# Stored sums for q and k, paired score adds and a replanned order in a Strassen-style attention and gated-MLP kernel

## The chip, the cores and the metric

The kernel runs on one core of one Trainium2 chip. The metric is device microseconds of one execution, lower is better; a version's time is the median of its runs. The core's engines are TensorE (PE, matmuls; PEld is its weight load), VectorE (DVE), ScalarE (ACT), GpSimd (POOL) and SyncE (SP). SP, POOL and ACT also issue DMAs, each in the order of its own queue; 16 DMA engines carry them.

## The reference

All inputs are bfloat16. `S` is 2048, `D` 1024, `F` 3584, 32 heads of 32, 8 offsets of step 2.

```python
xn = _layernorm(x)
qkv = (xn @ wqkv)                       # q, k, v by heads
idx = pos[:, None] - off[None, :]       # off = 0, 2, ... 14
kg, vg = k[:, :, idx_c], v[:, :, idx_c] # dilated window of 8 keys
logits = einsum("bhsd,bhswd->bhsw", q, kg) * scale   # masked where idx < 0
o = einsum("bhsw,bhswd->bhsd", softmax(logits), vg)
s = o @ wo
h = silu(xn @ w1) * (xn @ w3)
g = silu(h @ w2)
out = x + s * g
```

## The kernel before, in words

**Work and tiles.** The sequence is cut into four chunks of 512 rows (`CH`), two to a block (`BL` = 1024 rows, `NB` = 2 blocks; the code counts them as `b` = 0 and 1, the change's title calls the second "block 2"). Each large product is done on 2x2 blocks with seven products instead of eight, Strassen's way, so that some products take sums and differences of weights (`qkv_sums` L779, `w_sums` L1123, `w2_sums` L1212, `wo_sums`) and of activations (`xn_sums`, L461's helper `tt` issues them all on DVE). Within each block the order is: layer norm and the transposes of its output into `xT`; the q, k and v products (`qkv_pairs`); 14 steps of the gated up-projection (`up_step`, 256 columns of `w1` and `w3` each); the down-projection (`mlp_down`); and the output projection (`wo`). The attention itself has no matmul: scores, softmax and the weighted sum of values are elementwise DVE work that is placed beside PE's products, chunk by chunk (`scores` L866, `softmax`, `values`).

**Sums of weights.** In block 0 the sums are made on DVE; those that block 1 needs again are stored in DRAM from POOL's queue (`s_dram`, `s2_dram`, `t_dram`, `lt_dram`, and `sq_dram` for the q, k, v weights) and fetched by SP in block 1. For q, k and v the set `RL` (L354) says which of the three are stored: before, `RL = (2,)`, so v alone; the four sums of 128x2048 each of q and of k are made anew in block 1 from the weights, which are loaded in both cases.

**Scores.** `scores(c)` multiplies q with k shifted by each of the 8 offsets: two products of 128x2048 (`qk`), one add of 2048 (`qa`), one of 1024 (`qb`), one of 512 into `E` (`qc`). After four offsets `gather` brings the four partial sums of each head together by DMAs from `E` (two on POOL's queue, two on SP's), and `softmax` goes on with them. The `att` pool holds three buffers of 128x2048 for these and for the values.

**Buffers.** Weights and their sums share six buffers of 1 MB, the pool `r8` (the trace calls them `r`); `att` is `a`, `k2` (in the trace `k`) holds what ACT copies out of PSUM, `mm` is the eight PSUM banks. `h_sb` holds the up-projection's result, and before that, piece by piece, the `w2` weights whose sums go to `t_dram`, and parked q, k and v. A buffer is filled again when all users of what it held have ended, DMAs included.

**The order of the work.** Nothing is issued as the code runs. Each operation is recorded in `plan` with what it reads and writes, an assumed duration, and for DMAs their bytes. `limits` (L132) gives each a due time from the fixed order of PE's work. `simulate` (L158) then lets each engine take, of what is ready, the operation due first; DMAs share one pipe, each taking its bytes at one rate (`RATE` 3.3e5 bytes per us), the DMA's issue and 0.9 us. `replay` (L247) repeats this for each row of `ORDER`, which shifts due times of operations by number and moves PE's work, and the order that comes out last is what is issued; on the chip every engine keeps to it and waits by semaphores. All elementwise DVE work thus stands under one line, L461, all plain DMAs under L489, the matmuls of most products under L452, those of half width under L1099 and L1370, copies under L466, silu under L483 and the transposing DMAs under L654.

**The transposes.** `ln_turn` (L650) turns the next block's normalized rows into `xT` by transposing DMAs: four for chunk 2 on ACT's queue, four for chunk 3 on SP's. Each waits for a mark of the down-projection, after which its piece of `xT` is free.

Of the kernel before, what the change touches and what calls it, by code (L numbers as in the profile page):

```python
# [8 lines left out]
FP32 = mybir.dt.float32  # L9
# [25 lines left out]
class Op:  # L35
    __slots__ = ("eng", "emit", "rd", "wr", "occ", "lat", "table", "nbytes", "pred", "succ", "n",
                 "start", "done", "ready", "limit", "name", "late", "idx", "rate", "then", "need", "eta")


class Plan:  # L40
# [117 lines left out]
    def simulate(self):  # L158
# [24 lines left out]
        while left:  # L183
# [13 lines left out]
            if e == PE:  # L197
                o = ops[pes[pe_at]]
                pe_at += 1
                lag = T - o.need  # L200
            else:
                wait = None
                for i in sorted((i for i in ready[e] if ops[i].ready <= T), key=lambda i: (ops[i].limit, i)):
                    o = ops[i]
                    end = T + o.occ + (1.29 if o.table and o.table != table else 0.0)
                    hit = None
                    if e in self.look:
                        k = bisect.bisect_right(due[e], (T + 0.01, -1))
                        while k < len(due[e]) and due[e][k][0] < end - 0.05:
                            q = ops[due[e][k][1]]  # L210
                            k += 1
                            if q.start is None and q is not o and q.need < o.need:
                                hurt = end - max(q.need + lag, q.eta)
                                if hurt > 0.05 + self.look[e] * (q.eta - T):
                                    hit = q
                                    break
                    if hit is None:
                        break
                    wait = hit.eta if wait is None else min(wait, hit.eta)
                else:  # L220
                    free[e] = wait
                    continue
                ready[e].remove(i)
# [44 lines left out]
            o.emit()  # L268


ORDER = ((((403, 0.7), (402, -0.4), (438, 0.4), (402, -0.2), (409, -0.4), ), ()),
(((686, -1.1), (1076, 2.2), ), ((243, 242), )),
(((679, 2.4), (686, -1.6), (1076, 1.1), (680, 1.4), (680, 2.1), ), ((244, 242), )),
(((686, -0.4), (680, 1.1), (686, -0.6), ), ((245, 243), )),
(((998, -1.2), ), ()),
(((1077, 0.5), (1183, 1.2), ), ()),
(((1177, 0.7), (1178, 0.3), ), ()),
(((1183, 1.6), ), ()),
(((1181, 1.5), ), ((377, 376), )),
(((1077, 0.3), ), ((248, 247), )),  # L280
(((1284, -0.9), (1224, -0.8), (1128, 0.5), (1303, 1.2), ), ()),
(((1077, 0.2), (1200, 0.4), (714, 0.8), ), ((404, 403), )),
(((691, -0.3), ), ()),
(((1526, -1.5), (1529, 2), (1183, 0.8), (1183, 2), ), ()),
(((1548, 1.4), (1229, 0.2), ), ()),
(((694, 0.7), (993, 0.6), ), ((477, 471), )),
(((993, 0.9), (693, 0.6), (1545, 1.7), ), ((468, 472), )),
(((716, 0.2), (1199, 0.6), (715, -0.4), ), ()),
(((995, 0.6), ), ((251, 250), )),
(((1548, -0.6), (693, 0.2), (1231, 0.5), ), ((377, 371), )),  # L290
(((1181, 0.4), (691, -0.1), ), ((472, 471), )),
(((1554, 0.6), ), ()),
(((714, -0.4), (714, -0.1), (1463, 0.6), (1557, -1.2), ), ()),
(((702, 0.3), ), ()),
(((1545, -0.3), (693, 0.6), (686, 0.3), (1463, 0.6), (694, 0.7), ), ((478, 472), )),
(((1014, -1.3), (1222, 3.2), ), ()),
(((1526, 0.6), ), ()),
(((1520, 0.5), ), ()),
((), ((371, 370), (371, 370), )),
((), ((371, 370), (371, 370), )),  # L300
((), ((368, 371), (371, 370), )),
(((1446, 0.7), (1526, 0.6), (1470, 0.7), ), ()),
(((1245, -0.4), (1247, 0.9), (1247, 0.3), ), ((367, 371), )),
(((1212, 1.8), (1221, 1.7), ), ((371, 370), (364, 370), )),
(((1559, -0.3), ), ((369, 366), )),
(((1437, 0.8), (1575, -0.7), (1438, 1), (1528, 1), (1014, -1), ), ((485, 483), (366, 371), )),
(((2328, 2.3), ), ()),
(((1575, 2.8), (2022, 0.6), ), ((484, 483), )),
(((2085, 1), (1226, 0.7), (2087, -0.3), (1578, 1.8), ), ()),
(((1226, 0.8), ), ()),  # L310
(((1461, 2.7), ), ()),
(((1225, -0.3), (2093, -0.8), (2093, -0.6), ), ()),
(((1181, 0.6), (2090, 0.6), (1225, -0.4), ), ()),
(((2471, 0.3), ), ((475, 483), (483, 481), )),
(((1737, 0.7), (1519, -0.6), ), ((476, 475), )),
(((1737, 0.5), ), ((476, 483), (483, 481), )),
)
LAST = []

# [2 lines left out]
def kernel(  # L322
# [78 lines left out]
    LAST[:] = [plan]  # L401
    plan.pools = {
        "r8": [const.tile([P, 4 * D], BF16, name=f"r8_{i}") for i in range(6)],
        "att": [const.tile([P, 4 * CH], BF16, name=f"a4_{i}") for i in range(3)],
    }
    plan.wide = {"k2": const.tile([P, 8, CH], FP32, name="k2"), "mm": psum.tile([P, 8, CH], FP32, name="mm")}
    for n, t in plan.wide.items():
        plan.pools[n] = [t[:, i] for i in range(8)]

    ctx.enter_context(tc.manual_schedule())  # L410

# [74 lines left out]
    def dma(eng, name, o, a, rd, wr, kb, late=0.0):  # L486
        e = {SP: nc.sync, POOL: nc.gpsimd, ACT: nc.scalar}[eng]
        occ = {SP: 0.45, POOL: 0.58, ACT: 0.42}[eng]
        plan.op(eng, name, lambda: e.dma_start(out=o(), in_=a()), rd, wr, occ, 0.0, nbytes=kb * 1024, late=late)  # L489

    def sub_of(s, *idx):
        return (s,) + idx
# [157 lines left out]
    def ln_turn(c, st, xt, cell):  # L650

        half = c % 2
        eng, q, occ = (ACT, nc.scalar, 0.1) if c == 2 else (SP, nc.sync, 1.4)
        plan.op(eng, f"turn{c}_{st}", lambda: q.dma_start(  # L654
            out=xT[:, half, :, st * P:(st + 1) * P], in_=xrow(xt, st), transpose=True),
            [(xt, st), cell], xt_cells(half, 0, st) + xt_cells(half, 1, st), occ, 0.0, nbytes=256 * 1024)


    def qkv_load(t, split=False):
# [206 lines left out]
    def scores(c):  # L866
# [1045 lines left out]
```

## Time and profile before

| | |
|---|---|
| median of 3 runs | 713.04 us (712.6 to 715.51) |
| the profiled execution | 712.91 us, of which the span of its instructions is 711.1 |
| DMA | 165.68 MB, mean 233 GB/s |
| granted TensorE clock | 1.0 |
| matmul, 128x512 | drawn 379 ns long |
| DVE add, 128x2048 / 128x1024 / 128x512, all bf16 | 1213 / 680 / 413 ns |

The page's matmul ends are modelled: successive matmuls overlap as drawn, so a busy share near 100% says only that they follow one another closely. A DVE instruction is likewise drawn a little into the next one; start to start is what the engine needs. Times in the views are microseconds from the span's start.

### The profile page before, as it was taken

Reading aid. Unit: us, or ns where it says so; the run is one execution under the profiler, and the core shown is the slowest. Engines: PE = TensorE matmul, PEld = TensorE weight load, DVE = VectorE, ACT = ScalarE, POOL = GpSimd, SP = SyncE. Lnnn points to the kernel's source line nnn. Section 1 sums busy time; section 2 is a strip of 40 time slices with the busy share of each in tenths; the row PEclk is TensorE's granted clock in tenths of the full one; section 3 lists DMA queues with packets and bytes.
Section 4 is the critical chain, followed back from the end, with each engine's and each line's share of the span. In section 5 each row is a group of like instructions: output and inputs, shape, how many; then the busy total and the mean of one; then the engine's idle time right before and its main releaser. Section 6 shows DMA issues by size and latency. Waiting matters only on the chain.

```text
span 711.1 us, 9896 instructions
## 1 busy us (share of the span) xinstructions
PE 697.9 (98%) x3612; PEld 374.2 (53%) x3666; DVE 684.7 (96%) x859; ACT 397.6 (56%) x752; POOL 46.1 (6%) x89
## 2 busy tenths in 40 slices
PE   8999999999999999999999999999999999999997
PEld 5555545455555474644455554555555455656443
DVE  7999899999999999989999999999999999999965
ACT  7644565658565799512445455666866855322233
POOL 1011010112010010100010000000010010000000
PEclk9999999999999999999999999999999999999999
DMA  9999987666964779994466549973586575957502
GB/s 335 288 338 374 377 314 223 215 214 219 299 211 165 260 251 226 301 281 138 164 230 243 177 159 325 327 253 113 181 262 201 181 226 171 339 193 244 177 30 89
DMA packets 137087, 165.68 MB, mean 233 GB/s; under 512 B 16784, under 2 KB 112672, under 8 KB 131408
## 3 DMA queue, kind: packets, MB, share of 16 engines
q1 hardware_dynamic: 125552, 128.14, 56.5%
q0 software_dynamic: 6832, 35.41, 13.4%
q10 hardware_dynamic: 4656, 1.51, 1.3%
q8 instruction: 28, 0.46, 0.3%
q14 instruction: 19, 0.16, 0.1%
HBM read 113.12 MB, written 39.58 MB: 215 GB/s over the span
## 4 chain that ended last, share of the span: by engine, by line
PE 77%; DVE 14%; DMA 4%; issue 2%; ACT 2%; SPq 0%; DVEq 0%; ACTq 0%
PE mm L452 67%; PE mm L1099 5%; PE mm L1370 5%; DVE a L461 4%; DVE h_sb L461 3%; DVE r L461 3%; DMA h_sb<-in_B_w_dram 2%; DMA r<-in_B_w_dram 1%; DVE small L549 1%; DVE xs L461 1%; DMA r<-in_A_x_dram 1%; DVE r L565 0%; ACT k L466 0%; DVE k L461 0%; DMA xT<-r 0%
## 5 line engine op out<-in xcount | busy, mean ns | idle before, releaser
L452 PEld LDWEIGHTS <-r 128*128 128x128 f16 (+1 forms) x2068 | 219.4, 108 | 202.4 <-issue 4.9
L452 PE MATMUL mm<-xs,r 128*128 128x512 f16 x1280 | 300.3, 379 | 3.1 <-DVE h_sb L461 1.6
L452 PE MATMUL mm<-xT,r 128*128 128x512 bf16 (+2 forms) x747 | 173.2, 369 | 2.4 <-ACT small L554 0.2
L466 ACT COPY k<-mm 128x512 f32<-128x512 f32 (+1 forms) x226 | 124.3, 559 | 79.8 <-PE mm L452 72.8
L466 ACT COPY mm<-mm 128x512 f32<-128x512 f32 (+1 forms) x157 | 76.5, 491 | 108.3 <-PE mm L1099 34.0
L452 PE MATMUL mm<-r,h_sb 128*128 128x512 f16 (+1 forms) x583 | 129.2, 379 | 1.0 <-DMA r<-in_B_w_dram 0.5
L452 PEld LDWEIGHTS <-h_sb 128*128 128x128 f16 (+1 forms) x680 | 66.5, 98 | 80.5 <-issue 1.7
L461 DVE TENSOR_TENSOR a<-a,a 128x2048 bf16<-128x2048 bf16 (+3 forms) x70 | 78.4, 1122 | 0.2
L461 DVE TENSOR_TENSOR h_sb<-mm,k 128x1024 bf16<-128x1024 f32 x48 | 58.0, 1215 | 1.8 <-ACT k L466 1.1
L461 DVE TENSOR_TENSOR a<-qo,kT 128x2048 bf16<-128x2048 bf16 x48 | 57.7, 1215 | 0.1
L1099 PE MATMUL mm<-xT,r 128*128 128x256 f16 (+1 forms) x364 | 56.7, 273 | 0.0
L461 DVE TENSOR_TENSOR h_sb<-h_sb 128x1024 f16<-128x1024 bf16 (+7 forms) x74 | 53.4, 742 | 1.8 <-DMA h_sb<-in_B_w_dram 1.8
L461 DVE TENSOR_TENSOR r<-r,r 128x1024 f16<-128x1024 f16 (+7 forms) x62 | 50.0, 812 | 0.7 <-DMA xT<-r 0.5
L461 DVE TENSOR_TENSOR a<-E,vT 128x2048 bf16<-128x2048 bf16 x42 | 49.7, 1214 | 0.0
L1099 PEld LDWEIGHTS <-r 128*128 128x128 f16 (+1 forms) x364 | 35.6, 98 | 26.3
L461 DVE TENSOR_TENSOR k<-mm,k 128x1024 f32<-128x1024 f32 (+1 forms) x44 | 44.8, 1019 | 1.1 <-PE mm L452 0.8
L483 ACT ACTIVATE k<-k 128x512 bf16<-128x512 f32 x56 | 32.5, 626 | 20.1 <-DVE k L461 20.0
L483 ACT ACTIVATE h_sb<-mm 128x512 bf16<-128x512 f32 x60 | 36.4, 611 | 10.7 <-PE mm L452 9.3
L461 DVE TENSOR_TENSOR qo<-qo,a 128x2048 bf16<-128x2048 bf16 x32 | 38.8, 1213 | 0.0
L461 DVE TENSOR_TENSOR r<-r 128x1024 f16<-128x1024 bf16 (+4 forms) x73 | 38.1, 535 | 0.1
L461 DVE TENSOR_TENSOR h_sb<-h_sb,k 128x2048 bf16<-128x2048 bf16 x28 | 33.9, 1210 | 0.3 <-ACT k L483 0.3
L466 ACT CAST k<-mm 128x512 bf16<-128x512 f32 x56 | 31.5, 602 | 0.2 <-PE mm L452 0.2
(132 smaller groups left out, 563.9 us busy)
## 6 DMA issues: line engine op xcount, KB each, us to landing
r<-in_B_w_dram SPq DMA_DIRECT2D x42, 512.0 KB, 6.0
s_dram<-r POOLq DMA_DIRECT2D x14, 1024.0 KB, 5.1
r<-s_dram SPq DMA_DIRECT2D x14, 1024.0 KB, 5.0
r<-t_dram SPq DMA_DIRECT2D x15, 896.0 KB, 8.0
r<-in_A_wqkv_dram SPq DMA_DIRECT2D x10, 1024.0 KB, 7.1
r<-in_B_w_dram SPq DMA_DIRECT2D x11, 896.0 KB, 6.1
h_sb<-in_B_w_dram SPq DMA_DIRECT2D x14, 512.0 KB, 8.3
t_dram<-h_sb POOLq DMA_DIRECT2D x7, 1024.0 KB, 9.1
```

Source lines behind the costliest of these rows:

```text
L452: nc.tensor.matmul(cut(ps.ap()), lhsT=lhs[k](), rhs=cut(rhs[k]()), start=(first and k == 0), stop=(last and k == n - 1), skip_group_check= ...
L461: plan.op(DVE, name, lambda: fn(out=o(), in0=a(), in1=b()), rd, wr, occ, 0.08, late=late)
L466: plan.op(ACT, name, lambda: nc.scalar.copy(out=o(), in_=a()), rd, wr, occ, 0.11)
L483: plan.op(ACT, name, lambda: nc.scalar.activation(out=o(), in_=a(), func=ACTF.Silu), rd, wr, occ, 0.11, table="silu")
L549: plan.op(DVE, f"bn{c}_{st}_{h}", lambda h=h: nc.vector.bn_stats(out=stats[:, h, :], in_=xrow(xt, st)[:, h * 512:(h + 1) * 512]), ([("x ha ...
L1099: nc.tensor.matmul(half(pa[i].ap, n)(), lhsT=A[0][k](), rhs=B[0][k](), start=first and k == 0, stop=k == 1, skip_group_check=True)
L1370: nc.tensor.matmul(half(bank.ap, n)(), lhsT=a[k](), rhs=c[k](), start=first and k == 0, stop=k == NQ - 1, skip_group_check=True)
```

## The change

- `RL` becomes `(0,1,2)`: the sums for q and k are stored in DRAM in block 0, two stores of 1 MB each on POOL's queue, and fetched in block 1 by two DMAs of 1 MB each on SP's queue. The four sums each of q and k in block 1 are no longer made. The loads of the weights themselves stay.
- The three `att` buffers become one tile, so that two neighbours can be addressed together. In `scores`, for all offsets of chunks 2 and 3 and the first four of chunks 0 and 1, two offsets are taken together: products and `qa` as before, then one `qb` over both (128x2x1024) and one `qc` over both (128x2x4x128).
- The planner: each kind of DMA gets a factor on its bytes (`COST`), the fixed part of a DMA changes, `RATE` is 3.25e5, and a DMA is held back while the assumed pipe is over 4 us behind and the DMA is due in over 25 us.
- `ln_turn`: the transposes of chunk 3 also wait until all four of chunk 2 have landed; the assumed issue time and bytes are larger.
- `ORDER` is another list: 67 rows of shifts and moves instead of 46.

The two programs hold the same matmuls. In the new order of PE some groups of matmuls trade places in the first down-projection, the first output projection, the q and k products of block 1, one up step and the last output projection's neighbours; up to the first down-projection PE's order is the old one, and up to about 45 us that of DVE. On SP's queue seven instead of ten fetches of `w2` pieces stand ahead of the v weights; five of the 14 stand behind fetches for later up steps. On POOL's queue three instead of seven stores of `w2` sums stand ahead of the second store of up-projection sums; the four new stores stand first, third and so on among them.

```diff
+BACKLOG, SPARE = 4.0, 25.0
...
                     o = ops[i]
+                    if o.nbytes and pipe - T > BACKLOG and o.need + lag - T > SPARE:
+                        wait = T + 0.5 if wait is None else min(wait, T + 0.5)
+                        continue
...
-                pipe = max(pipe, T + occ + 0.9) + o.nbytes / o.rate
+                pipe = max(pipe, T + min(occ, 0.45) + 0.66) + o.nbytes / o.rate
...
-    RL = (2,)
+    RL = (0,1,2)
...
-        "att": [const.tile([P, 4 * CH], BF16, name=f"a4_{i}") for i in range(3)],
     }
-    plan.wide = {"k2": const.tile([P, 8, CH], FP32, name="k2"), "mm": psum.tile([P, 8, CH], FP32, name="mm")}
+    plan.wide = {"att": const.tile([P, 3, 4 * CH], BF16, name="a4"), "k2": const.tile([P, 8, CH], FP32, name="k2"), "mm": psum.tile([P, 8, CH], FP32, name="mm")}
...
+        for part, cost in COST:
+            if name.startswith(part):
+                kb = kb * cost
+                break
...
+    COST = (("turn", 1.7), ("w1.", 1.17), ("w3.", 1.17), ("putk", 1.14), ("putq", 1.35), ("put_s", 0.87), ("put_l", 1.43),
+            ("s_dram", 0.8), ("s2", 1.7), ("L", 0.58), ("E", 0.69), ("out", 0.65), ("t2_", 1.15), ("wo", 1.2),
+            ("getv", 1.21), ("get_l", 1.15), ("movev", 1.48))
...
-        eng, q, occ = (ACT, nc.scalar, 0.1) if c == 2 else (SP, nc.sync, 1.4)
+        eng, q, occ = (ACT, nc.scalar, 0.1) if c == 2 else (SP, nc.sync, 2.3)
...
-            [(xt, st), cell], xt_cells(half, 0, st) + xt_cells(half, 1, st), occ, 0.0, nbytes=256 * 1024)
+            [(xt, st), cell] + [("turned", k) for k in range(NST) if c == 3],
+            xt_cells(half, 0, st) + xt_cells(half, 1, st) + [("turned", st)] * (c == 2), occ, 0.0, nbytes=int(1.7 * 256 * 1024))
...
+        two = None
         for w in range(W):
...
+            if c >= 2 or w < 4:
+                if w % 2 == 0:
+                    two = plan.pair("att", f"p{c}_{w}", f"p{c}_{w}")
+            else:
+                two = None
             for jh in range(2):
-                p_t = plan.slot("att", f"p{c}_{w}_{jh}")
+                p_t = two[w % 2] if two and not jh else plan.slot("att", f"p{c}_{w}_{jh}")
...
+            if two and w % 2 == 0:
+                continue
+            if two:
+                v = lambda two=two: two[0].both().rearrange("p w (j n) -> p w j n", j=4)
+                tt(f"qb{c}", add, lambda v=v: v()[:, :, 0:2], lambda v=v: v()[:, :, 0:2], lambda v=v: v()[:, :, 2:4], two, two, 2048, True)
+                tt(f"qc{c}", add, lambda w=w: E[:, :, w - 1:w + 1, :].rearrange("p q w n -> p w q n"),
+                   lambda v=v: v()[:, :, 0].rearrange("p w (q n) -> p w q n", n=P),
+                   lambda v=v: v()[:, :, 1].rearrange("p w (q n) -> p w q n", n=P),
+                   two, [("E", x, sq, r) for x in (w - 1, w) for sq in range(4) for r in range(NR)], 1024, True)
+                if w % 4 == 3:
+                    gather(c, w // 4)
+                continue
...
-    RATE = 3.3e5
+    RATE = 3.25e5
```

More of the change, by code (lines that the diff above doesn't have):

```diff
@@ L268, in run @@
             o.emit()
[L271 to L292, printed above, removed]
@@ L316 @@
-(((1737, 0.5), ), ((476, 483), (483, 481), )),
+ORDER = (((), ((29, 26), (29, 26), (29, 26), (29, 26), )),
+((), ((27, 26), (27, 26), )),
+((), ((27, 26), (27, 26), )),
+(((647, -0.7), ), ()),
+(((684, 1.9), ), ()),
+(((684, 1.8), ), ()),
+((), ((243, 242), )),
+(((1076, 0.5), (684, 1.1), ), ((244, 242), )),
+(((684, 3.3), (684, 7.4), ), ((245, 243), )),
+(((1004, 1.1), (1175, 3.5), (1077, 0.7), ), ()),
+(((695, -0.4), ), ()),
+(((1074, 3.8), (1074, 5.3), (1077, 1.4), ), ((248, 247), )),
+(((1077, 0.3), ), ((251, 250), )),
@@ new lines @@
+(((1193, 10.9), (1193, 10.3), ), ()),
+((), ((375, 377), )),
+(((1012, 0.6), ), ((370, 369), )),
+(((1220, -0.3), ), ()),
+(((1175, 10.8), (1006, 0.2), (1175, 3.6), ), ((368, 371), )),
+(((1276, 0.4), ), ()),
+(((1126, 7.6), ), ((405, 403), )),
+(((1305, 4.1), (1350, -4.2), (1311, 3.1), (1277, 4.6), (1174, 0.3), ), ((423, 417), )),
+(((1347, 1.8), ), ((422, 417), )),
+(((1174, 0.4), (997, 8.3), (1344, 1), (1304, 0.4), ), ()),
+((), ((427, 426), )),
+(((1347, 1.4), ), ()),
+((), ((419, 417), )),
@@ new lines @@
+(((1174, 0.8), ), ()),
+(((1176, 0.6), (1012, -0.6), ), ()),
+(((1173, 0.3), (1004, 2), (1173, 0.4), (1174, 0.5), ), ()),
+(((1012, -0.4), (1012, -0.2), (1012, -0.5), (1173, 0.8), ), ()),
+(((1175, 0.5), ), ((377, 376), )),
+(((1012, -0.4), (1012, -0.2), ), ((369, 368), )),
+(((1472, 6.6), (1345, 0.5), (1343, 0.3), ), ()),
+(((1387, -0.6), (1343, 0.3), ), ((435, 434), )),
+((), ((27, 26), (27, 26), )),
+((), ((25, 26), (25, 26), )),
+((), ((458, 455), )),
+((), ((456, 455), (456, 455), )),
+((), ((458, 456), )),
@@ L317 @@
+((), ((457, 455), (455, 453), (457, 455), )),
+(((1729, 4.5), (1679, 1.1), (2323, 0.9), ), ((594, 592), )),
+(((2326, -0.3), (2334, 0.5), ), ()),
+(((2312, 0.8), (1875, 0.4), ), ()),
+((), ((593, 596), (598, 596), )),
+(((1755, 0.5), (1752, 11.9), (1743, 15.3), (1878, -0.3), (1862, 0.6), (1748, 4.1), ), ((597, 595), )),
+(((2310, 0.5), (2312, 0.3), ), ((761, 760), )),
 )
```

46 lines of the change are left out of this document (22 added, 24 removed).

## The prediction

> **What bounds the kernel now.** The page comes first: the busy shares, then how many records each engine left.
>
> ```profile
> span 711.1 us, 9896 instructions
> PE 697.9 (98%) x3612; PEld 374.2 (53%) x3666; DVE 684.7 (96%) x859; ACT 397.6 (56%) x752; POOL 46.1 (6%) x89
> q1 hardware_dynamic: 125552, 128.14, 56.5%
> q0 software_dynamic: 6832, 35.41, 13.4%
> PE 77%; DVE 14%; DMA 4%; issue 2%; ACT 2%; SPq 0%; DVEq 0%; ACTq 0%
> ```
>
> TensorE (PE) and VectorE (DVE) are both nearly full. 77% of the chain that ended last is PE, so a DVE instruction that goes is worth only the hole in PE that it caused. What holes are there? The view of stretches of 15 us gives PE, PEld, DVE, ACT, POOL busy, the clock, the DMA share and GB/s.
>
> ```profile
> 0.00:15.00 15.00, 12.65 (x104) 8.42 (x106) 11.40 (x31) 10.81 (x25) 2.90 (x13) 1.00 0.91 325
> 30.00:45.00 15.00, 14.21 (x66) 7.88 (x66) 15.00 (x20) 7.84 (x15) 1.12 (x2) 1.00 0.94 335
> 60.00:75.00 15.00, 14.95 (x71) 8.77 (x70) 14.93 (x18) 7.89 (x15) 1.06 (x2) 1.00 1.06 398
> 75.00:90.00 15.00, 14.82 (x68) 7.87 (x69) 13.20 (x18) 8.04 (x14) 1.59 (x3) 1.00 1.09 368
> 90.00:105.00 15.00, 13.75 (x73) 7.04 (x72) 14.96 (x26) 9.27 (x19) 3.25 (x6) 1.00 0.83 306
> 150.00:165.00 15.00, 14.95 (x79) 7.71 (x79) 13.88 (x23) 9.74 (x21) 1.11 (x3) 1.00 0.46 150
> 330.00:345.00 15.00, 14.36 (x67) 6.47 (x67) 14.83 (x21) 5.74 (x12) 1.07 (x2) 1.00 0.63 213
> 345.00:360.00 15.00, 14.89 (x69) 8.25 (x70) 15.00 (x25) 8.02 (x12) 0.00 (x0) 1.00 0.16 51
> 360.00:375.00 15.00, 14.32 (x64) 8.03 (x64) 13.79 (x18) 6.19 (x12) 2.18 (x4) 1.00 0.86 294
> 705.00:720.00 15.00, 2.28 (x15) 1.22 (x13) 2.34 (x7) 0.66 (x2) 0.00 (x0) 0.94 0.16 52
> ```
>
> PE is idle for 711.1 - 697.9 = 13.2 us. The first 15 us hold 2.35 of it (15 - 12.65) and the end 3.82 (6.1 - 2.28). Some 7.0 us are left between, and part of that is no idle time: 3666 weight loads stand against 3612 matmuls, so 54 records are missing.
>
> ```profile
> 377.11 1.89 PE L452 MATMUL mm<-xT,r 128*128 128x512 bf16 x8
> 378.84 1.89 PE L452 MATMUL mm<-xs,r 128*128 128x512 f16 x8
> L452 PE MATMUL mm<-xs,r 128*128 128x512 f16 x1280 | 300.3, 379 | 3.1 <-DVE h_sb L461 1.6 <-DVE qo L461 0.7 <-ACT k L466 0.3
> ```
>
> Eight matmuls take 378.84 - 377.11 = 1.73 us, 0.216 each, while a record is drawn 0.379 long. A missing record thus leaves a hole of 2 x 0.216 - 0.379 = 0.05 us, and 54 of them 2.9. Real holes are 7.0 - 2.9 = 4.1 us; the drawn length hides up to 0.379 - 0.216 = 0.16 in each of about ten, so some 5.7. The hole at 30 to 45 us (0.74 + 0.16) stays, because the instructions of PE and DVE stand in the same order there in both built programs. **About 4.8 us can be won at all.** PE does 3666 matmuls of the same shapes before and after, and the granted clock is 1.00 up to the last slice.
>
> **The change part by part.** *Sums kept.* In the second half `qkv_sums` no longer makes four sums each for q and k: 8 TENSOR_TENSOR of 128x2048. A merged row gives the pitch, and next to it stand the small ones of the scores.
>
> ```profile
> 320.34 2.35 DVE L461 TENSOR_TENSOR a<-qo,kT 128x2048 bf16<-128x2048 bf16 x2
> 322.61 0.68 DVE L461 TENSOR_TENSOR k<-mm,k 128x512 f32<-128x512 f32 x1
> 324.68 0.68 DVE L461 TENSOR_TENSOR a<-a 128x1024 bf16<-128x1024 bf16 x1
> 325.28 0.68 DVE L461 TENSOR_TENSOR k<-mm,k 128x512 f32<-128x512 f32 x1
> 332.82 0.42 DVE L461 TENSOR_TENSOR E<-a 128x512 bf16<-128x512 bf16 x1
> 333.16 2.35 DVE L461 TENSOR_TENSOR a<-qo,kT 128x2048 bf16<-128x2048 bf16 x2
> 372.35 2.48 DVE L461 TENSOR_TENSOR r<-r,r 128x2048 f16<-128x2048 bf16 x2
> ```
>
> Two of 2048 take 322.61 - 320.34 = 2.27, so 1.135 each; 1024 takes 0.60 (325.28 - 324.68), 512 takes 0.34. The 8 sums free 9.1 us of DVE.
>
> *Scores in pairs.* Twelve pairs of offsets (four each in chunks 2 and 3, two each in 0 and 1) merge two adds of 1024 into one of 2048 and two of 512 into one of 1024: 12 x (1.20 - 1.135 + 0.68 - 0.60) = 1.7 us. A pair of two-row outputs stands in no row; from no gain (0) to a slower form at twice the new instructions (12 x 1.735 = 21 us more) is the range, and I take the 1.7, since every row with 128-element inner runs goes at this pitch. DVE is freed of 10.8 us in all, 9.1 of it between 340 and 378 us.
>
> What is that worth? PE there loses 0.64 (330 to 345), 0.11 and 0.68 (360 to 375), less 0.05 to 0.1 a stretch for missing records, plus 0.16 each that the drawn length hides: about 0.75 and 0.75. The first ends with ScalarE (the row at 342.98 below), so I credit half; the second is DVE's (0.36 us behind h_sb at 364.25, and 372.35 + 1.2 meeting the matmuls at 373.63), so all of it. **1.1 us.** The rest of the 9.1 us becomes idle DVE time: below, PE is full from 375 on.
>
> *What the kept sums cost.* Four more stores of 1 MB on POOL's queue before 60 us and four more fetches on SP's at 335 to 370.
>
> ```profile
> sq_dram<-r POOLq DMA_DIRECT2D x2, 1024.0 KB, 7.9
> r<-sq_dram SPq DMA_DIRECT2D x2, 1024.0 KB, 5.4
> kT<-park_k SPq DMA_DIRECT2D x1, 1024.0 KB, 11.7
> 342.98 1.89 PE L452 MATMUL mm<-h_sb 128*128 128x512 f16 x8 [0.59 <-ACT k L466]
> 344.71 1.89 PE L452 MATMUL mm<-r,h_sb 128*128 128x512 bf16 x8
> 349.89 1.89 PE L452 MATMUL mm<-h_sb,qo 128*128 128x512 f16 x8
> 356.79 1.89 PE L452 MATMUL mm<-xs,r 128*128 128x512 f16 x8
> 364.25 5.79 PE L452 MATMUL mm<-xs,r 128*128 128x512 f16 x24 [0.36 <-DVE h_sb L461]
> 373.63 3.65 PE L452 MATMUL mm<-xs,r 128*128 128x512 f16 x16
> 343.60 1.23 SPq L489 DMA_DIRECT2D a<-E  x2
> 356.24 6.86 SPq L489 DMA_DIRECT2D out_dram<-r  x5
> 363.46 1.40 SPq L489 DMA_DIRECT2D r<-in_A_wqkv_dram  x2
> ```
>
> The fetches fill buffers that the output projection leaves. By the new order PE wants the first q sums at the place of the row at 349.89 and the second at 356.79. The second buffer is free after the matmuls of 344.71 (346.6), and the issue stands behind the gathers at 343.60, done 344.8: 346.6 + 5.4 = 352.0, 4.8 us early. The first is free once the projection's first 16 matmuls and the sums of its weights are done, 32 matmuls and the 0.59 before 346.6, so about 339.1; 339.1 + 5.4 = 344.5, 5 us early likewise. The k sums' first buffer is free when its last q matmuls end, two groups of eight after 356.79 (360.3), and its fetch stands behind the output stores (to 363.1) and one weight fetch on SP (about 364): 364 + 5.4 = 369.4 against 373.6, 4 us early. DMA share there is 0.16 to 0.86. So they cost nothing at 5.4 each.
>
> The stores fall where the DMA engines are full (shares 0.94 to 1.09). By q0's row a stored MB takes 0.134 x 711.1 / 35.41 = 2.7 us of all 16 engines: 4.19 MB take 11.3 us. But in the new order three instead of seven stores of w2 sums stand ahead of the second store of up-projection sums, four (4.19 MB) fewer, and the last five of the fourteen w2 fetches (2.5 MB) move behind later up steps. So the rush is no larger, and what moves (11.3 us, and 2.6 MB x 0.565 x 711.1 / 128.14 = 8 us) lands after 105 us, where the row at 150 shows a share of 0.46. I take 0.
>
> *The planner.* Timing by kind, the hold and the ORDER are no work on the chip; they act through the order. Four of the seven sets of w2 sums (16 adds of 1024, 9.6 us of DVE) leave the stretch before 100 us. In the old one DVE stood still behind a w2 fetch there, and PE soon after behind DVE:
>
> ```profile
> L461 DVE TENSOR_TENSOR h_sb<-h_sb 128x1024 f16<-128x1024 bf16 x28 | 18.1, 683 | 1.8 <-DMA h_sb<-in_B_w_dram 1.8
> ```
>
> 15 - 13.20 = 1.8 us of DVE at 75 to 90, then 1.25 us of PE at 90 to 105. Less 0.05 and plus 0.16, **1.35 us** goes if the set that waits is moved; late next is then the step's own adds, one of 1.2 us. Scores move ahead in exchange, so DVE's sum up to 300 us is unchanged.
> Four transposes on SP's queue now wait until the four of ScalarE's queue have landed; behind them on SP stand t_dram and wo fetches.
>
> ```profile
> L654 ACTq DMA_TRANSPOSE xT<-r x4: 1247/1296/3267, 267.2 to 273.4; - x4
> L654 SPq DMA_TRANSPOSE xT<-r x4: 1238/2576/8107, 292.3 to 306.5; - x4
> ```
>
> From 273.4 to 292.3 there are 19 us, more than the slowest landing quoted (11.7), so the wait costs 0; without that cover each us would hold up those fetches, and the projection's matmuls after them.
>
> *New holes.* 67 rows of shifts and swaps replace 46; PE's order differs in a dozen places. The cost lies between 0 and a doubling of the 4.8; the nearest rows are single waits of 0.4 to 0.6 (364.25, 342.98). I take one: 0.5.
>
> **Sum.** 712.91 (span 711.1 and 1.8 around it) - 1.1 - 1.35 + 0.5 = 710.96; the median is 0.13 over the profiled run, so **711.1 us**.
>
> **A rule against it.** The stretch at 60 us moves 398 GB/s. "DMA: Bandwidth & Descriptors" of the Trainium skill, section Specifications, puts HBM's limit per core at about 358 GB/s; by it 4.19 MB more would last 11.7 us where none is free. The trace has gone past that figure, so it is no hard wall here, but the direction is that of rival E.
>
> **The rivals.**
> B, *late fetches*: the wait for DVE becomes a wait for DMA. If the fetches land as slowly as the slowest of their kind (11.7), the q sums come at 339 + 11.7 = 350.7 (0.8 late) and 358.3 (0.7 more), the k sums at 375.7 (2.1 to 2.7 late). It decides from a landing of about 10 us. The 1.1 is then lost and 4.2 added: 712.9 + 4.2 - 1.35 = **715.8**; the SP queue being in order, a late gather adds directly, so half of this case lies over 716.6. For it: 7.9 us for such a store. Against: the idle DMA at 345 to 360. Chance 0.20.
> C, *it does not do what it says*: PE's holes are moved, not closed: **713.0**. For: 10.8 us of DVE is off the end's path. Chance 0.10.
> D, *all holes close*: 712.9 - 4.8 = **708.1**. Chance 0.16.
> E, *no room*: the added stores hold the weights of the first up steps. 11.3 us, less the 2.5 free at 90 to 105 (0.17 x 15), is 8.8: **721.7**. It decides if the moved 4.19 MB don't stay behind 105 us. Chance 0.09.
>
> **How the numbers follow.** My forecast has 0.45, reaching 709.3 to 713. A measurement of this kernel tells about 0.5% (3.6 us) from no change: 709.5 to 716.6 counts as the same. Faster: D and a sliver of the forecast, 0.19. Slower: E and half of B, 0.20. Same: 0.61. The range goes from just under D's 708.1, the floor, to 717.5, inside B's upper half; E and some 0.05 of B lie outside.
>
> **What would show it.** Right: eight fewer sums of 2048 in DVE, about 10 us less busy; the stretches 90 to 105 and 360 to 375 at 14.9 for PE; r<-sq_dram x6 near 5 to 6 us. Wrong: PE or DVE waiting for r<-sq_dram; adds of 128x2x1024 or E of 1024 slower than 1.22 and 0.68; PE waiting for r<-in_B_w_dram between 60 and 200 us; new holes in the up steps, where filler adds stand ahead of those that free a bank. A PE busy time far below 698 would upset the whole argument.

## The result, and the profile after

| | before | after |
|---|---|---|
| median | 713.01 us (712.3 to 715.51, 22 runs) | **709.04 us** (707.35 to 713.38, 22 runs) |
| ratio of after to before | | 0.9952, 95% interval 0.9939 to 0.9966 |
| the profiled execution | 712.91 us, span 711.1 | 709.42 us, span 707.6 |

The forecast was 711.1 with a range from 708.0 to 717.5. The time lies in the range, two thirds of the way from the forecast to rival D ("all holes close", 708.1). The runs after fall into two groups, 14 at 707.4 to 709.4 and 8 at 711.5 to 713.4; the median stands in the first. The page of the changed kernel, its busy shares, two DMA queues and the shares of the chain of waits:

```profile
span 707.6 us, 9945 instructions
PE 699.7 (99%) x3666; PEld 374.1 (53%) x3666; DVE 674.8 (95%) x827; ACT 399.0 (56%) x752; POOL 48.4 (7%) x93
q1 hardware_dynamic: 126128, 132.33, 58.6%
q0 software_dynamic: 7408, 39.61, 15.0%
PE 83%; DVE 9%; DMA 3%; issue 2%; ACT 1%; SPq 1%; DVEq 0%; POOL 0%; ACTq 0%
```

DVE lost 9.9 us of work (684.7 to 674.8), each of the two DMA queues gained 4.2 MB, and DVE's share of the chain fell from 14% to 9%. No matmul record is missing this time, so PE's idle time can be read straight: 707.6 - 699.7 = 7.9 us, against 13.2 - 2.9 = 10.3 before. The stretches of 15 us of the changed kernel, with the columns of the prediction's fence (PE, PEld, DVE, ACT, POOL busy, clock, DMA share, GB/s):

```profile
30.00:45.00 15.00, 14.16 (x67) 7.72 (x66) 15.00 (x19) 7.34 (x14) 2.15 (x4) 1.00 1.03 398
90.00:105.00 15.00, 15.00 (x81) 7.67 (x79) 14.92 (x22) 10.51 (x21) 3.27 (x6) 1.00 0.98 325
330.00:345.00 15.00, 15.00 (x71) 6.80 (x70) 14.93 (x22) 6.05 (x11) 0.24 (x1) 1.00 0.72 263
345.00:360.00 15.00, 15.00 (x72) 8.45 (x70) 14.96 (x25) 8.56 (x14) 0.83 (x2) 1.00 0.74 254
360.00:375.00 15.00, 15.00 (x71) 9.00 (x70) 10.03 (x13) 8.18 (x15) 2.19 (x4) 1.00 1.02 346
```

PE is full at 90 to 105 and from 330 to 375, where the prediction looked for it. DVE is now idle for 5.0 us at 360 to 375, where it was for 1.2; at 330 to 360 DVE is as full as ever, because the new order put other work there. What PE still waits for, in the changed kernel (us in total, times, longest), and below it the same view of a second execution of the same kernel (label a_again):

```profile
PE mm L460 <- DVE k L458: 1.3, 1, 1.3
PE mm L478 <- DMA r<-in_A_wqkv_dram: 1.0, 2, 0.6
PE mm L478 <- DVE qo L487: 0.8, 1, 0.8
PE mm L478 <- DVE r L487: 0.7, 1, 0.7
PE mm L478 <- ACT k L492: 0.5, 1, 0.5
```

```profile
PE mm L478 <- ACT small L641: 1.6, 1, 1.6
PE mm L460 <- DVE k L458: 1.3, 1, 1.3
PE mm L665 <- DVE r L599: 0.7, 1, 0.7
PE mm L478 <- DMA r<-in_A_wqkv_dram: 0.3, 1, 0.3
```

All but the ACT k wait (at 249 us) lie in the first 50 us, and the second execution has no hole behind 25 us at all. So the gain is simple to place. Eight holes of before (near 97, 246, 300, 342, 364, 368, 373 and 564 us, 4.7 us by the spacing of successive matmuls) and two of 0.2 (near 86 and 366) became one of 0.7 (near 249, the old one near 246) or none. The first 50 us gave some of it back: the 251st of the 3666 weight loads starts at 45.82 us before, at 47.10 in the profiled execution after, and at 45.99 in the second, so 1.3 us in the one and 0.2 in the other. Which part of the change closed them is not simple, and is what the experiments are for.

### The profile page after: what moved, and what is told of

Its sections match the earlier page's. It is cut to its first block, busy times and chain, and to the rows that moved or that the text cites. A ratio compares the mean times of both kernels' runs of the same rounds, so it can differ in the third digit from the quotient of the medians.

```text
span 707.6 us, 9945 instructions
## 1 busy us (share of the span) xinstructions
PE 699.7 (99%) x3666; PEld 374.1 (53%) x3666; DVE 674.8 (95%) x827; ACT 399.0 (56%) x752; POOL 48.4 (7%) x93
## 4 chain that ended last, share of the span: by engine, by line
PE 83%; DVE 9%; DMA 3%; issue 2%; ACT 1%; SPq 1%; DVEq 0%; POOL 0%; ACTq 0%
PE mm L478 73%; PE mm L1423 6%; PE mm L1152 4%; DVE r L487 2%; DVE a L487 2%; DMA s_dram<-r 1%; DVE qo L487 1%; DVE h_sb L487 1%; DMA r<-in_A_wqkv_dram 1%; DVE k L487 1%; DMA r<-in_A_x_dram 1%; DMA xT<-r 0%; DVE mm L487 0%; DVE small L583 0%; ACT k L492 0%
## 5 line engine op out<-in xcount | busy, mean ns | idle before, releaser
L478 PE MATMUL mm<-xT,r 128*128 128x512 bf16 (+2 forms) x788 | 178.8, 370 | 1.7 <-DMA r<-in_A_wqkv_dram 1.0
L487 DVE TENSOR_TENSOR a<-a 128x2048 bf16<-128x2048 bf16 (+7 forms) x106 | 107.1, 1011 | 0.7
L487 DVE TENSOR_TENSOR r<-r,r 128x1024 f16<-128x1024 f16 (+7 forms) x56 | 42.8, 768 | 3.0 <-DMA xT<-r 1.5
L509 ACT ACTIVATE k<-k 128x512 bf16<-128x512 f32 x56 | 32.2, 622 | 22.9 <-DVE k L487 22.9
L487 DVE TENSOR_TENSOR r<-r 128x1024 f16<-128x1024 bf16 (+4 forms) x71 | 35.9, 514 | 0.8 <-DMA r<-in_A_wqkv_dram 0.8
```

The costliest lines, as they stand in the source:

```text
L478: nc.tensor.matmul(cut(ps.ap()), lhsT=lhs[k](), rhs=cut(rhs[k]()), start=(first and k == 0), stop=(last and k == n - 1), skip_group_check= ...
L487: plan.op(DVE, name, lambda: fn(out=o(), in0=a(), in1=b()), rd, wr, occ, 0.08, late=late)
L509: plan.op(ACT, name, lambda: nc.scalar.activation(out=o(), in_=a(), func=ACTF.Silu), rd, wr, occ, 0.11, table="silu")
```

## Experiments

Ratios are to the kernel before on the same chip (its median there 713.25 to 713.81). Labels with b_ start from the kernel before, those with a_ from the changed one. Except in a_nohold, the order is planned as in that kernel, and then single operations are left out, split, moved or issued behind another; everything else keeps its place. Sizes of holes are taken from the spacing of successive matmuls, so they are a little longer than the idle time in the brackets of a row.

| label | median us | ratio to before (95%) |
|---|---|---|
| b_stores | 724.0 | 1.0141 (1.0128 to 1.0154) |
| b_kept | 729.87 | 1.0226 (1.0212 to 1.024) |
| b_w2late | 712.64 | 0.9984 (0.9973 to 0.9995) |
| a_anew | 716.46 | 1.0039 (1.0026 to 1.0052) |
| a_k_anew | 712.03 | 0.9995 (0.9976 to 1.0014) |
| a_single | 709.11 | 0.9962 (0.9941 to 0.9982) |
| a_nohold | 723.74 | 1.0148 (1.0122 to 1.0173) |
| a_fetch_twice | 724.86 | 1.0185 (1.0153 to 1.0218) |
| a_store_late | 712.21 | 0.9984 (0.9974 to 0.9995) |
| a_lighter | 709.52 | 0.9953 (0.9935 to 0.9971) |
| a_again (the changed kernel) | 709.53 | 0.9957 (0.9939 to 0.9974) |
| a_gate | 729.94, one run | |

**The stores alone, in the old order (b_stores).**

```diff
 # before.py, qkv_sums, first half: behind the last sum of each buffer of q and k
+nc.gpsimd.dma_start(out=sq_dram[t][i], in_=r8v(S[i], FP16))      # nothing reads them
```

> The kernel before in its own order, plus the four stores of 1 MB (q and k sums in the first half) on POOL's queue right behind the sums; nothing fetches them. Theory (the stores cost next to nothing, the DMA engines catch up later): 713 to 714, and the hole in PE near 26 us that the changed kernel shows (+0.86, PE waits for DVE r 0.7) is here too if that store makes it. Rival E (the stores hold the first up steps' weights, all the more as all seven stores of w2 sums stand in the rush here): 716 to 722, with PE waiting for DMA r<-in_B_w_dram between 60 and 105 us.

724.0, so +10.3 us: the direction and nearly the size of rival E, 8.8 in the prediction. It came by another route than E's: PE waited for v's weights, not for those of the first up steps. The hole at 26 us was here too (PE waits 0.9). Three kernels, two views each. First SP's queue before those loads in the kernel before, in b_stores and in the changed kernel (start, us, engine, line, operation, count), then the DMA table of the stretch from 30 to 65 us with the median landing of v's two weight loads, in the same order:

```profile
23.44 6.16 SPq L489 DMA_DIRECT2D h_sb<-in_B_w_dram  x10
```

```profile
23.51 10.28 SPq L495 DMA_DIRECT2D h_sb<-in_B_w_dram  x10
```

```profile
23.75 5.77 SPq L519 DMA_DIRECT2D h_sb<-in_B_w_dram  x7
```

```profile
r<-in_A_wqkv_dram SPq DMA_DIRECT2D x2, 1024.0 KB, 8.3
```

```profile
r<-in_A_wqkv_dram SPq DMA_DIRECT2D x2, 1024.0 KB, 20.7
```

```profile
r<-in_A_wqkv_dram SPq DMA_DIRECT2D x2, 1024.0 KB, 12.4
```

The loads are issued at 41 to 42 us in all three. With ten w2 fetches ahead and the four new stores beside them they take 20.7 us, with seven and the same stores 12.4, with ten and no such stores 8.3. The price of it in b_stores, PE's matmuls and the stretch around them:

```profile
62.91 2.86 PE L458 MATMUL mm<-xT,r 128*128 128x512 bf16 x8 [3.40 <-DMA r<-in_A_wqkv_dram]
66.89 3.60 PE L458 MATMUL mm<-xs,r 128*128 128x512 f16 x8 [1.11 <-DVE r L467]
```

```profile
60.00:75.00 15.00, 9.45 (x30) 4.34 (x31) 9.40 (x10) 3.44 (x7) 1.06 (x2) 0.77 1.08 380
```

PE is busy for 9.45 of 15 us, with the DMA engines full (share 1.08); and behind the wait the eight matmuls take 3.60 us where they take 1.73 to 1.89 elsewhere (granted clock 0.77). Of that more in the last section. Between 59 and 72 us b_stores loses about 9 us in this way, 2 of them in half-paced matmuls, and 1 more at 26. As far as these three tables go, the stores are nearly free in the new order because it takes w2 fetches and w2 sums out of the same microseconds; the new order with ten fetches ahead was not run.

**Kept sums in the old order (b_kept).** As b_stores, with the eight sums replaced by fetches:

```diff
 # before.py, second half, q and k
-qs0, qs1, qs3, qs2 (4 x 128x2048 on DVE)
+nc.sync.dma_start(out=r8v(S[i], FP16), in_=sq_dram[t][i])   # issued behind the last user of the buffer
```

> The kernel before in its own order, with the four stores and with the eight sums of 2048 in the second half replaced by four fetches of 1 MB, each emitted as soon as the last user of its buffer is emitted. No pairs, no new plan. Theory of the prediction (the sums are worth the holes from 330 to 375 us, 1.1 us, and the stores nothing): 711.5 to 712.5, PE at 14.9 in the stretches from 330 to 375. Rival B (fetches late): above 713, PE waiting for DMA r<-sq_dram. Rival from the trace of the changed kernel (the holes from 330 to 400 were all DVE's, 2.4 us in all): 710.5 to 711.

729.87, 5.9 over b_stores, though DVE has 8.4 us less to do (676.3 busy against 684.7). Rival B's sign held in part: PE waits for `r<-sq_dram`, but only 0.6 us. About 2 us of the difference lie in the first 80 us of the two profiles, where both kernels have the same instructions. Most of the rest is one hole in the second half. SP's queue and PE in b_kept:

```profile
374.82 0.34 SPq L808 DMA_DIRECT2D r<-sq_dram  x1
375.21 1.04 SPq L498 DMA_DIRECT2D r<-in_A_wqkv_dram  x2
```

```profile
385.12 6.30 PE L461 MATMUL mm<-xT,r 128*128 128x512 bf16 x16 [4.26 <-DMA r<-in_A_wqkv_dram]
```

PE does not wait there for the fetch but for the weights queued behind it: the fetch stood on SP until its buffer came free at 374.8, and the two loads with it. This is rival B's "SP queue being in order" clause, with a weight load in the gather's place, and it is a cost of the place I gave the fetch, not of fetching. The holes that the sums themselves made near 364 to 373 us are gone in b_kept; the one near 342, which ends with ScalarE, is still there (1.0 us at 353).

**The changed order without the kept sums (a_anew), and with q's alone (a_k_anew).**

```diff
 # after.py, order frozen
-put_sq0_0, put_sq0_1, put_sq1_0, put_sq1_1        # stores, first half
-sq0_0, sq0_1, sq1_0, sq1_1                        # fetches, second half
+qs0, qs1 (q) behind qc1; qs3, qs2 (q) behind sq0_1's place
+qs0, qs1 (k) behind pb1; qs3, qs2 (k) behind sq1_1's place
 # a_k_anew: the same for k only; q is stored and fetched as in after.py
```

> The changed kernel with its order frozen, but the eight sums of 2048 for q and k made again on DVE in the second half in the place of the fetches, and no stores of them in the first. Theory of the prediction (the sums fill DVE and hold PE up at 330 to 375 us): +1 to +2.5 there, less 0.8 at 26 us if the store makes that hole: 709 to 711. Rival (the order, not the sums, closed these holes): 708 to 708.5, PE full at 330 to 375 with DVE near 15 us in each stretch.

> The changed kernel, same order, q's sums kept as in it, but k's four sums made again on DVE in the second half and not stored in the first. Theory (the hole of 3.7 us with q and k both made anew comes from q's sums, which stand where DVE has no slack; k's stand in the 5 us that DVE idles between 360 and 375): PE full up to 370, at most a hole of 1 behind it, and with two stores less in the rush at 35 to 60 us 707.5 to 709.5. If k's stores are what lets the changed kernel's time jump by 4 us in a third of its runs, no run here lies above 711. Rival (k's sums are as dear as q's): a hole over 2.5 us between 365 and 385, 712 to 714.

716.46 and 712.03, against 709.04 and 709.53 for the changed kernel. Both theories of a_anew put the sums too cheap: +7.4 by the medians, not +2.5. In a_anew, four stretches and the waits of PE:

```profile
90.00:105.00 15.00, 15.00 (x82) 7.72 (x80) 14.92 (x22) 9.54 (x20) 3.25 (x6) 1.00 0.94 312
330.00:345.00 15.00, 15.00 (x71) 6.93 (x70) 14.90 (x20) 6.09 (x12) 1.08 (x2) 1.00 0.70 239
345.00:360.00 15.00, 13.37 (x62) 7.52 (x61) 14.97 (x25) 6.08 (x10) 0.00 (x0) 1.00 0.25 73
360.00:375.00 15.00, 13.08 (x48) 6.38 (x48) 10.15 (x12) 6.55 (x11) 2.18 (x4) 0.77 0.68 217
```

```profile
PE mm L484 <- DVE h_sb L493: 5.4, 3, 3.6
```

q's four sums stand at 342 to 348 us, where DVE is full; the adds that free PE's banks come 4.5 us later, PE waits 3.6 for them, and then runs some fourteen matmuls at half pace (2.9 us more).

The first two stretches matter as much. Up to 355 us a_anew has none of the holes of before but the one at 33: its 1851st weight load starts at 350.65 us, against 354.42 before. So the new order closes the holes near 97, 246, 300 and 342 without the kept sums and is 3.8 us ahead there; it then loses 7.2 between 357 and 391 us, where the sums stand in the places I gave them. The kernel before makes the same sums in its own places and loses 1.3 us near 364 to 373.

For k's sums I had counted on DVE's 5 idle us. In a_k_anew, DVE and PE:

```profile
367.31 3.88 DVE L829 TENSOR_TENSOR r<-r,r 128x2048 f16<-128x2048 bf16 x3 [3.66 <-DMA r<-in_A_wqkv_dram]
```

```profile
374.65 1.89 PE L484 MATMUL mm<-xs,r 128*128 128x512 f16 x8 [1.53 <-DVE h_sb L493]
```

The sums need k's weights, which PE wants only later and which land at 367: DVE idles for 3.7 of its 5 us, then does the sums ahead of the adds that PE waits for. +2.5 us, so the theory of the idle 5 us fell and the rival (k's are dear too) held in the time, though not by one hole of over 2.5 us: there are two, of 1.7 and 1.5. Nor did the long runs vanish (up to 717.7).

**The pairs undone (a_single).**

```diff
 # after.py, scores: same order, each paired add issued as two
-add(out=v[:, :, 0:2], in0=v[:, :, 0:2], in1=v[:, :, 2:4])
+for k in range(2): add(out=v[:, k, 0:2], in0=v[:, k, 0:2], in1=v[:, k, 2:4])   # and so for qc
```

> The changed kernel, same order, with each of the twelve paired adds issued as two single ones (24 more DVE instructions, 1.7 us more DVE by the rows). Theory (DVE is the bound up to 300 us only through single holes): 0 to +1.7 over the changed kernel, 709 to 710.8. Rival (the pairs are hidden work, or their gain is lost to strides): within 0.3 of it.

709.11: no difference. The page of a_single, to be held against the changed kernel's 674.8 of DVE:

```profile
PE 699.6 (99%) x3666; PEld 374.4 (53%) x3666; DVE 675.6 (96%) x851; ACT 398.6 (56%) x752; POOL 48.3 (7%) x93
```

The pairs are worth 0.8 us of DVE, half of the 1.7 costed, and nothing in time.

**The hold removed (a_nohold).**

```diff
-BACKLOG, SPARE = 4.0, 25.0
+BACKLOG, SPARE = 1e9, 25.0
```

> The changed kernel planned anew without the hold on transfers that are due late; PE's order stays, DVE's and the queues' change. Theory (the hold takes the w2 fetches out of the rush from 40 to 90 us, and so closes the holes from 50 to 105 us): PE's holes there come back, 711 to 715. Rival (the hold is not what matters, the shifts in the list are): 708.5 to 710.

723.74, further off than the theory. PE's first loss in a_nohold:

```profile
29.48 3.24 PE L478 MATMUL mm<-xT,r 128*128 128x512 bf16 x8 [2.96 <-DVE r L487]
```

DVE there waits 3.8 us for the transposes (`xT<-r`), and further holes of 2.2, 1.5, 0.7, 1.0 and 0.9 follow up to 175 us. The comparison is lopsided: the shifts of `ORDER` were fitted with the hold in place, so this shows that order and hold belong together, not what a hold is worth by itself.

**Where the fetches' margin ends (a_fetch_twice).** In the changed kernel the fetches take 5.1 us, those of the q sums are issued at these times, and PE's first use of either is at these:

```profile
r<-sq_dram SPq DMA_DIRECT2D x6, 1024.0 KB, 5.1
```

```profile
338.14 0.34 SPq L519 DMA_DIRECT2D r<-sq_dram  x1
345.79 0.52 SPq L519 DMA_DIRECT2D r<-sq_dram  x1
```

```profile
348.34 1.89 PE L478 MATMUL mm<-xs,r 128*128 128x512 f16 x8
355.24 1.89 PE L478 MATMUL mm<-xs,r 128*128 128x512 f16 x8
```

338.14 + 5.1 = 343.2 leaves 5.1 us, 345.79 + 5.1 leaves 4.3; the prediction had 5 and 4.8.

```diff
 # after.py: behind each of the four fetches
+nc.sync.dma_start(out=r8v(S[i], FP16), in_=sq_dram[t][i])   # the same once more
```

> The changed kernel with each of the four fetches of kept sums issued twice, so that the buffer is good only when the second has landed, about 10 to 11 us after the first issue instead of 5. Margins in the changed kernel's trace: 5.0, 4.3, 6.8, 7.9 us. Rival B's price (late from a landing of some 10 us): PE waits for r<-sq_dram by 0.5 to 1.5 at the q sums and little at the k sums, 710 to 712.5. If the margins are larger than the trace makes them: 709, no such wait.

724.86, so 15.8 us over the changed kernel where 1 to 3.5 were expected. SP and PE in a_fetch_twice:

```profile
336.22 9.64 SPq L525 DMA_DIRECT2D r<-sq_dram  x2
```

```profile
351.01 3.05 PE L484 MATMUL mm<-xs,r 128*128 128x512 f16 x8 [4.44 <-DMA r<-sq_dram]
360.71 2.53 PE L484 MATMUL mm<-xT,r 128*128 128x512 bf16 x8 [2.64 <-DMA r<-sq_dram]
390.29 3.60 PE L484 MATMUL mm<-xT,r 128*128 128x512 bf16 x8 [3.52 <-DMA r<-sq_dram]
```

The second fetch is issued only when the first has landed, so SP stands still for 9.6 us and everything queued behind it is late too. The three holes, the last at the k sums, come to 11 us, and each is lengthened by half-paced matmuls (3.05, 2.53 and 3.60 for the first eight), 6 us together. Rival B's mechanism is real, but this is not B's price: a single fetch that lands slowly would not hold SP, and the second fetch landed near 351 us, almost 15 us after the first was issued, where B had 11.7.

**The first store later (a_store_late), two transfers later (a_lighter).** The profiled run of the changed kernel has a hole of 0.9 (0.7 as drawn) at 26 us that before lacks, with a store of q sums issued beside the transposes at 22.9; and 13 of its 34 runs, the dear runs, lie above 711, at 711.4 to 713.6, the others at 707.4 to 710.1.

```diff
 # a_store_late: POOL's queue
-put_sq0_0  ...  put_sq0_1
+put_sq0_1, put_sq0_0
 # a_lighter: SP's and POOL's queue
-w2q (7th) ... wqkv2_0, wqkv2_1        -t_dram (2nd), put_sq1_1
+wqkv2_0, wqkv2_1, w2q (7th)           +put_sq1_1, t_dram (2nd)
```

> The changed kernel, same order, but the first store of q sums is issued on POOL's queue only behind the second, some 6 us later. Theory (that store, beside the transposes, makes the new hole of 0.86 near 26 us): 708 to 708.4, DVE no longer waiting 1.5 us for DMA xT<-r there. Rival (the hole comes from the new plan's order of loads and transposes): unchanged, 709.

> The changed kernel with two transfers of the first 60 us moved back: the seventh w2 fetch (0.5 MB, wanted at about 61 us) behind the loads of v's weights, the second store of w2 sums (1 MB) behind the last store of k's sums. All else in its order. Theory (the spread of the changed kernel's times comes from the full DMA engines before 60 us, through the stores of q's sums that must have read their buffers before DVE and the v weights may write them): fewer dear runs, at most 1 in 6 above 711 where the changed kernel has 1 in 2.5; median 708 to 708.6. Rival (the spread is set before these transfers, or the moved ones collide elsewhere): as many dear runs as in the changed kernel, 709 to 710.

> The changed kernel itself, run and profiled again, for the spread of its times: 14 of its 22 runs lay at 707.4 to 709.4 and 8 at 711.5 to 713.4. Theory: in a dear run a transfer of the first 60 us lands late enough for one hole of over 2.5 us in PE, behind which PE runs at half its pace for some microseconds, as it did behind every such hole of the other kernels here; if this profile is of a dear run, both stand in it before 70 us, and the rest is full. Rival (the clock is lowered by the long full load): half-paced matmuls without a hole ahead of them, at any place.

a_store_late's hole at 26 went and a dearer one came. a_again has none at 26 either, so that hole comes and goes from run to run. Over all profiles it stands in 5 of the 10 that have a q store at 22 to 24 us (after, a_k_anew, a_nohold, b_stores, b_kept) and in none of the 4 that have not; that fits the store as its cause and does not prove it. DVE and PE in a_store_late:

```profile
42.94 1.22 DVE L493 TENSOR_TENSOR r<-r,r 128x2048 f16<-128x2048 bf16 x1 [2.63 <-DMA sq_dram<-r]
```

```profile
45.95 3.06 PE L484 MATMUL mm<-xs,r 128*128 128x512 f16 x8 [2.48 <-DVE qo L493]
48.81 2.45 PE L484 MATMUL mm<-xT,r 128*128 128x512 bf16 x8
```

A store holds its source: k's sums may not be written over q's before q's have been read, and 6 us later was too late. PE lost 2.6 us and then 1.5 at half pace, and all its runs now lie at 711.2 to 713.4, which is where the changed kernel's dear runs lie. That fits the theory that those have such a hole, but no profile of a dear run of the changed kernel was caught, and a_lighter, made to thin them out, left them as many (5 of 11 above 711). **Where the dear runs lose their 4 us stays open.**

**The w2 set that waits, moved (b_w2late).**

```diff
 # before.py, DVE's order near 78 us
-w2s(25), qc0, w2s(26), qk0, w2s(27), qk0
+qc0, qk0, qk0, w2s(25), w2s(26), w2s(27)
```

> The kernel before with three w2 sums of one set (the one that waits 1.8 us for its weights at 78.6 us, and two after it) moved behind the two score products that stood after them; all else in the old order. Theory of the prediction: DVE's wait goes and PE's hole near 99 us with it, -1.35: 711.3 to 711.9. Rival (the DVE time gained is used up before PE needs it, or the hole has another cause): 712.7 to 713.3 with the hole at 99 still there.

712.64, 1.0 us under the kernel before (0.4 to 1.9 by the interval), so nearer the theory's 1.35 than the rival's nothing. Its runs reach from 710.9 to 713.8, and the profiled one is among the longest (713.38). DVE and PE of it:

```profile
74.42 1.29 DVE L467 TENSOR_TENSOR r<-r 128x1024 f16<-128x1024 bf16 x2 [2.25 <-DMA r<-in_B_w_dram]
81.98 2.13 DVE L467 TENSOR_TENSOR h_sb<-h_sb 128x1024 f16<-128x1024 bf16 x3
```

```profile
100.06 1.02 PE L458 MATMUL mm<-xs,r 128*128 128x512 f16 x4 [1.20 <-DVE h_sb L467]
```

The moved set waits no more, but in this execution DVE stood 2.25 us for the first up step's weights instead, so the wait passed to another transfer, and PE's hole is the old one, 1.20 as drawn. Whether the hole closed in the shorter runs, of which there is no profile, stays open.

**Holes made with idle work (a_gate).**

```diff
 # after.py, six up steps of the second half, behind uh
+n x nc.vector.reciprocal(out=idle, in_=idle)    # idle is 128x64, n = 4, 4, 5, 6, 8, 10; result unused
```

> The changed kernel with idle work for DVE (reciprocals of 128x64, some 0.5 us each, their result unused) in six steps of the second up-projection: 4, 4, 5, 6, 8 and 10 of them, 24 us apart, so that PE, which waits for DVE there, gets holes of about 1.5 to 5 us. Theory (PE runs at half its pace after a hole of over about 2.5 us, and the length of the slow stretch doesn't follow the hole's): no doubled matmuls behind the holes up to 2.2, 5 to 12 of them (1.1 to 2.5 us more) behind those from 2.6 on. Rival (the slow stretches of the other kernels had to do with their DMA load or place, not with the hole): none here, the cost of each hole is its length.

Matmuls went at half pace behind the holes of 2.5 and 5.4 us (about six each), and not behind those of 1.3, 1.7, 2.7 and 3.7. Four stretches of a_gate (the eighth column is the clock):

```profile
505.00:520.00 15.00, 12.62 (x58) 5.87 (x57) 14.14 (x18) 8.15 (x17) 2.18 (x4) 0.89 0.67 211
535.00:550.00 15.00, 12.31 (x64) 6.16 (x64) 14.90 (x19) 8.27 (x17) 1.09 (x2) 1.00 0.42 134
565.00:580.00 15.00, 14.54 (x74) 7.21 (x74) 15.00 (x19) 13.21 (x23) 0.00 (x0) 1.00 0.38 124
595.00:610.00 15.00, 14.99 (x71) 7.34 (x71) 14.46 (x14) 9.92 (x21) 0.00 (x0) 0.90 0.43 135
```

The stretches behind the holes of 2.5, 2.7, 3.7 and 5.4 us stand in this order. Neither side holds: slow stretches come here behind idle work alone, without a late transfer, and at a DMA share of 0.43 as at 0.67, but the hole's length does not decide it. It is one run with one profile.

No version here beats the changed kernel; a_single and a_lighter equal it.

## Why the prediction was right or wrong, point by point

- **What bounds the kernel: right.** PE's holes were all there was to win. It said 4.8 us "can be won at all"; the ten holes behind 45 us came to 5.1, and a_again has none left there. By its own marks the time fell just below the 709.5 where it set "faster", to which it gave 0.19.
- **DVE freed of 10.8: 9.9.** The eight sums are 9.1 as costed (9.9 less a_single's 0.8; 8.4 in b_kept); the pairs are 0.8, not 1.7, and worth nothing in time.
- **"1.1 us" for the holes at 330 to 375: mis-sized.** They were 2.0 by the spacing of matmuls (0.75, 0.52, 0.21, 0.25, 0.30), and all went. Crediting the first, which "ends with ScalarE", by half lost 0.4; in b_kept, without the sums, it is still there, and in a_anew, with them, the new order has closed it. The other 0.5 is a miscount: 360 to 375 holds four holes, and the sum added what the drawn length hides only once.
- **"1.35 us" for the hole at 97: the size right, the reason not shown.** The hole closed in the changed kernel, and in a_anew. Moving the set that waits (b_w2late) took 1.0 us off the time but did not close the hole in the execution profiled.
- **Holes credited nothing: the step that failed.** Those near 86, 246, 300 and 564 us (0.24, 0.43, 0.70, 0.36) had no edit beside them, and the sum left them as they were. The new order closed them all in a_again and all but the one at 246 (0.7 at 249) in the profiled run. With the 0.9 above that is 2.6 us too little credited.
- **"New holes", 0.5: too low for the profiled run, too high for the other.** The first 50 us cost 1.3 in the one, most of it the hole at 26, and 0.2 in the other. So errors of both signs met in the profiled run: 2.6 of gain not credited, against 0.8 of loss not charged here and the 0.7 left at 249. That leaves 1.1 of the 1.5 us by which 709.42 lies under the sum's 710.96; another 0.3 was gained behind the last weight load. That the total came so near is in part luck.
- **"The hole at 30 to 45 us stays": it did** (14.16 for PE) in the profiled run. In the second execution, which lost 0.9 us more before 25 us, it was gone.
- **Stores at 0: nearly right, and for the reason given as far as shown,** that w2 fetches and w2 sums leave the rush; what they may cost is the hole at 26. In the old order they cost 10.3 us (b_stores), half-paced matmuls included. That this is near rival E's 8.8 is no proof of E's sum: the weights that came late were v's. The limit of "A rule against it" was passed again: the changed kernel moved 398 GB/s from 30 to 45 us, with the stores in it.
- **Fetches at 0: right**, margins 5.1 and 4.3 against 5 and 4.8, and no wait of PE for them in either profile. Rival B's price was not measured by itself; fetches that are later than B's and hold the queue cost 15.8 (a_fetch_twice). What B's sum lacked is the half-paced matmuls behind each hole.
- **The transposes' wait at 0:** no wait of PE names them; it was not tried alone.
- **The planner's edits "are no work on the chip": true, but they carry the result.** The order without the kept sums is 0.4% slower than before (a_anew), the kept sums without the order are 2.3% slower (b_kept), both together are 0.5% faster. But a_anew is 3.8 us ahead of before up to 355 us, so most of the gain is the order's and comes without the kept sums; these are needed behind 355 us, in the places that sums and fetches had here. Neither half was planned anew for itself. A list fitted to the changed planner with the sums still made anew might keep the 3.8, and then the kept sums are worth little: this rival was not run. Which of the planner's edits does it, the hold, the costs by kind or the list, is open too.

## What to carry to other kernels

Where two engines are full, an edit that frees one is worth the holes that the order can close with it, and all holes, not only those beside the edit, are up for closing when the order is made anew: keep "all close" as a full rival. When an edit and a new order come together, run each alone and see where in the span it gets ahead, not only the time at the end. A store or fetch called free should come with the transfer that makes room for it, named, and with what stands behind it on its queue. The cost of a late transfer is not its lateness: count the queue that it blocks.

## What the runs showed of the hardware that was not expected

**A hole of over 2.5 us in PE is often paid twice.** In the experiments other than a_gate, nine holes of 2.6 to 4.6 us (spacing of matmuls, behind 25 us) were each followed, at once or within 2 us, by 3 to 14 matmuls at half pace, 0.43 instead of 0.216 us each: 0.7 to 2.9 us more. No hole of up to 2.2 us that stood by itself was. In a_gate two of four holes of 2.5 us and more were, of 2.5 and 5.4 us, and those of 2.7 and 3.7 were not. Stretches of 15 us with such matmuls show granted clocks of 0.71 to 0.98. This is part of why the experiments that failed cost more than any theory gave: 2 of 10 us in b_stores, 6 of 16 in a_fetch_twice. The Trainium skill, in "TensorE: Matmul & The Clock Gate", section "Part 1: The HAM clock gate", says that the array's clock is halved after an idle window of some 3.4 us and comes back after as long of work, the window running freely. A free window would let a hole fall well or badly, as in a_gate; but a hole of 2.5 us was enough here, which is shorter than the window stated.

**A kernel can become faster and less steady.** Before, runs lie within 712.1 and 715.7 throughout; the changed kernel's lie at 707.4 to 710.1 or at 711.4 to 713.6, and in 11 of the 13 dear ones the granted clock is below 1 (0.995 to 0.999), in 1 of the 21 others. a_store_late's profile, with its hole of 2.6 us and half-paced matmuls, has 0.998. That fits holes of this kind in the dear runs, without showing them.
